# Rewriting the opening of a fused attention and FFN kernel engine by engine

## The chip, the cores and the metric

The kernel runs on one core of a Trainium2 chip. The core has a matrix engine (TensorE, PE in the profile), a vector engine (DVE), a scalar engine (ACT), GpSimd (POOL) and SyncE (SP), each with its own instruction queue that runs in order; 16 DMA engines move data. DMAs are issued by POOL (in software, the only kind here that converts fp32 to bf16 on the way) and by SP (in hardware). The metric is the time of one execution on the device in microseconds (us); lower is better. Three runs of the kernel before took 458.5, 458.74 and 458.5 us, so the median is 458.5.

## The reference

Attention over 8 batches, 12 heads, 448 positions and 64 columns a head, with a squared ReLU in place of the softmax; then a two-layer FFN with an exact GELU over the 3584 rows of 768 columns. Everything comes in and goes out in fp32.

```python
scores = scale * np.matmul(q, k.transpose(0, 1, 3, 2))      # scale = 1/8
attn = np.maximum(scores, 0.0) ** 2 / S                      # S = 448
x = np.matmul(attn, v)                                       # then heads side by side: 3584 x 768
h = x @ w_in                                                 # 768 x 2048
g = 0.5 * h * (1.0 + erf(h / np.sqrt(2)))
out = g @ w_out                                              # 2048 x 768
```

## The kernel before

**Layout.** The score matmul needs q and k with the head's 64 columns on the partitions (`qT`, `kT`, two heads side by side on 128 partitions). q and k arrive with positions on the partitions: `load` (line 71) issues on POOL, for a batch or for a quad of four heads, two DMAs of k into `nk`, one of q into `nq`, and two of v for each quad into `vt`. Each partition holds several neighbouring positions, so that the DMA's runs are long. `permute` (line 115) then copies `nk` to `pk` in two pieces (lines 127 and 128) and `nq` to `pq` (line 129), on DVE, which brings the columns of two heads together. After that they are transposed, in one of two ways:

- `prep_pe` (line 133), a quad at a time: the permutes, then eight PE transposes of k into one PSUM tile (line 140) that is copied to `kT` (by ACT at line 148 in batch 0, by DVE at line 150 otherwise), then eight of q, copied to `qT` by DVE (line 150). The PSUM tiles come from the pool `f_pp` with two buffers, which the FFN matmuls use too.
- `prep_dma` (line 152), a whole batch at a time: the permutes, then eight DMA transposes on SP, four of q and four of k (line 157).

`nk`, `nq`, `pk` and `pq` have one buffer each: the loads of the next batch wait for the permutes of the batch before, and the permutes wait for its transposes. `qT` and `kT` have two buffers.

**Steps.** A batch is 3 quads of 7 steps. `qk_step` (line 166) makes four score matmuls of 64 keys against 448 queries, one ReLU with the scale on ACT (line 181), and the square on DVE (line 183). `av_step` (line 186) makes four matmuls with v (line 193); after a quad's seventh step DVE copies the two PSUM banks to `xT` (line 204). These banks have two buffers in all, so the next quad's first `av_step` waits for the copies. The list `lag` holds the steps whose `av_step` is still to come.

**FFN.** `ffn1` (line 207) is one of 16 column blocks of the first product for one batch: 6 matmuls (line 212) and a GELU on ACT (line 219). `ffn2` (line 223) is half of one 128-row tile of the second product: 16 matmuls (line 228) and a copy on DVE (line 236); after the second half SP stores the tile (line 246).

**Order.** Every engine runs its instructions in the order in which the program emits them. `weave` (line 291) emits the score steps of a batch in pairs and puts FFN pieces ("atoms", with estimated costs 1.14 and 2.6) between the pairs in proportion; `prep` names what is emitted ahead of the pair that begins at step `l`. Batch 0 has no FFN work beside it (lines 324 to 337): one score step after the other, the `av_step` four steps behind. Batch 1 has the `ffn1` atoms of batch 0, batch b the `ffn1` atoms of b-1 and `ffn2` atoms of the pair of batches before.

**Preparation before the change.** Quad 0 of batch 0 is prepared at the start (line 323), quad 1 after step 1, quad 2 after step 5, quad 0 of batch 1 after step 16, each as one block: permutes, transposes, copies. Quads 1 and 2 of batch 1 are prepared in the same way ahead of steps 0 and 6 of batch 1's weave. Batch 2 is prepared by DMA transposes at the end of that weave (line 355), batch 3 ahead of step 12 of batch 2 (line 377), all later batches ahead of step 0 of the batch before (line 380), the loads of the batch after that ahead of step 4 (line 382).

Of the kernel before, what the change touches and what calls it, by code (L numbers as in the profile page):

```python
# [33 lines left out]
def kernel(  # L34
# [9 lines left out]
    nc = tc.nc  # L44
# [21 lines left out]
    f_pp = pool("f_pp", 2, PS)  # L66


    nq, nk, vt = {}, {}, {}

    def load(b, g0, g1):
# [6 lines left out]
        nc.gpsimd.dma_start(nk[b][:KB, h0:h1, :], kk[:, :, : 4 * D])  # L78
        nc.gpsimd.dma_start(nk[b][KB:, h0:h1, : 3 * D], kk[:, :, 4 * D :])  # L79
        nc.gpsimd.dma_start(  # L80
            nq[b][:, h0:h1, :], q[b, h0:h1].rearrange("h (p c) d -> p h (c d)", c=NC)
        )
        if b == 0 and g0 == 0:
            nc.gpsimd.affine_select(
                out=ident, in_=ident, compare_op=mybir.AluOpType.not_equal, fill=1.0,
                base=0, pattern=[[-1, 128]], channel_multiplier=1,
            )
# [27 lines left out]
    def permute(b, g0=0, g1=G):  # L115

        h0, h1 = 4 * g0, 4 * g1
# [5 lines left out]
        pq = perm[b][0].rearrange("p c (h d) -> p h c d", d=D)  # L123
        pk = perm[b][1].rearrange("p c (h d) -> p h c d", d=D)
        sq = nq[b].rearrange("p h (c d) -> p h c d", d=D)
        sk = nk[b].rearrange("p h (c d) -> p h c d", d=D)
        nc.vector.tensor_copy(pk[:, h0:h1, :3], sk[:, h0:h1, :3])  # L127
        nc.vector.tensor_copy(pk[:KB, h0:h1, 3], sk[:KB, h0:h1, 3])  # L128
        nc.vector.tensor_copy(pq[:, h0:h1], sq[:, h0:h1])  # L129

    ident = const.tile([128, 128], BF16, tag="ident", name="ident")

    def prep_pe(b, g):
        permute(b, g, g + 1)
        for w, rows in ((1, (128, 128, 128, 64)), (0, (KC,) * 4)):
            tp = f_pp.tile([128, 2, S], BF16, tag="f", name="tp")
            for j in range(2):
                off = 0
                for t, r in enumerate(rows):
                    nc.tensor.transpose(  # L140
                        tp[:, j, off : off + r],
                        perm[b][w][:r, t, bass.ts(2 * g + j, 128)],
                        ident[:r, :r],
                    )
                    off += r
            dst = get_T(b)[w][:, 2 * g : 2 * g + 2, :]
            if b == 0 and w == 1:
                nc.scalar.copy(dst, tp)  # L148
            else:
                nc.vector.tensor_copy(dst, tp)  # L150

    def prep_dma(b):
        permute(b)
        for w, rows in ((0, (KC,) * 4), (1, (128, 128, 128, 64))):
            off = 0
            for t, r in enumerate(rows):
                nc.sync.dma_start_transpose(  # L157
                    get_T(b)[w][:, :, off : off + r], perm[b][w][:r, t, :]
                )
                off += r  # L160
# [25 lines left out]
    def av_step(b, g, i):  # L186
        if i == 0:
            pav[b, g] = [av_pp.tile([128, NB], F32, tag="av", name="pav") for j in range(2)]
        a2 = asq.pop((b, g, i))
        for j in range(2):  # L190
            r = slice(64 * j, 64 * j + 64)
            for e in range(2):
                nc.tensor.matmul(  # L193
                    pav[b, g][j][64 * e : 64 * e + 64, :S],
                    vt[b][r, g, e, bass.ts(i, D)],
                    a2[r, e, :],
                    start=(i == 0),
                    stop=(i == NK - 1),
                )
# [49 lines left out]
    def f1(b):  # L249
        return [(1.14, ffn1, (b, m)) for m in range(KF)]  # L250
# [55 lines left out]
    def later(fn, *a):  # L306
        return lambda: fn(*a)
# [4 lines left out]

    nc.scalar.activation(warm, warm, AF.Gelu)
    load(0, 0, 1)
    load(0, 1, 2)
    load(0, 2, 3)
    load_win(0)
    load_win(1)

    ctx.enter_context(tc.manual_schedule())  # L320


    prep_pe(0, 0)
    for l, st in enumerate(steps(0)):
        qk([st])
        if l == 1:
            prep_pe(0, 1)
        if l == 5:
            prep_pe(0, 2)
            load(1, 0, 1)  # L330
            load_win(2)
            load(1, 1, 2)
            load_win(3)
            load(1, 2, 3)
        if l == 16:
            prep_pe(1, 0)
        run_av(4)


    s1, a0 = steps(1), f1(0)  # L340
    qk(s1[:2])
# [3 lines left out]
        s1[4:],  # L345
        a0[:14],
        {
            0: [later(prep_pe, 1, 1)],
            6: [
                later(prep_pe, 1, 2),  # L350
                later(load, 2, 0, G),
                later(load_wout, 0),
                later(load_wout, 1),
            ],
            16: [later(prep_dma, 2)],
        },
    )
    while lag:
        run_av(0)
    run(a0[14:])  # L360

    for b in range(2, B):
        x1, x2 = f1(b - 1), f2(b - 2)
        todo = steps(b)
        if b == 2:
            run(x1[:6])
            atoms = mix(x1[6:], x2)
        else:
            atoms = x2[:2] + mix(x1, x2[2:])
            if b % 2 == 0:  # L370
                todo = todo[1:]
            elif b + 1 < B:
                todo = todo + steps(b + 1)[:1]
        prep = {}
        if b == 2:
            load(3, 0, G)
            prep[12] = [later(prep_dma, 3), later(load, 4, 0, G)]
        else:
# [39 lines left out]
```

## Time and profile before

| | |
|---|---|
| median of three runs | 458.5 us |
| the profiled execution | 459.15 us |
| its span, first to last instruction | 457.4 us |
| mean granted clock of PE | 0.949 |
| PE busy | 401.9 us (88%) |
| DVE busy | 183.4 us (40%) |
| ACT busy | 212.6 us (46%) |
| POOL busy | 61.7 us (13%) |

The profile shows one execution. Its page groups the instructions; the trace behind it can be asked for stretches of time, single tiles, waits, and the chain of work that ended last. A line such as "82.18 9.26 PE L212 MATMUL psh<-xT,win_sb ... x48" says: from 82.18 us, over 9.26 us, 48 matmuls of line 212 that write `psh` and read `xT` and `win_sb`. A bracket at the end gives the idle time of the engine before that line and what ended it. SPq is the instruction queue of SP, where DMAs are issued; a line "DMA kT<-pk" is the transfer itself. The granted clock is the share of its full speed that PE was given: 1.00 is full, 0.50 half.

### The profile page before, as it was taken

To read this page: it belongs to the slowest core of one execution; us is meant where nothing else is said; L and a number is where in the kernel's file an instruction comes from. 1 tells how busy PE (TensorE), PEld (TensorE's weight loads), DVE (VectorE), ACT (ScalarE), POOL (GpSimd) and SP (SyncE) were. 2 spreads that over 40 slices of the span, in tenths; PEclk is the share of its full clock that TensorE was granted. 3 is DMA by queue.
4 is the path that set the end of the run, shared out by engine and by line. 5 is a ranking of instruction groups with operands and counts; after the bars stand their busy time and mean duration, and the time that the engine had idled before them with its cause. 6 is when DMAs were issued, how large, how long until landed. Compare 5 with 4: busy or idle time off the path is not lost.

```text
span 457.4 us, 7385 instructions
## 1 busy us (share of the span) xinstructions
PE 401.9 (88%) x3104; PEld 202.2 (44%) x3104; DVE 183.4 (40%) x319; ACT 212.6 (46%) x301; POOL 61.7 (13%) x95
## 2 busy tenths in 40 slices
PE   2677789804998599999999998999999999999995
PEld 1323344402543255445444544454545554455563
DVE  1566565201465253435434642464344344310021
ACT  2574467401555234655566464555555556412200
POOL 8361051410023040005000500000000000000000
PEclk9975899975999799999999999999999999999999
DMA  9999059997119999209951894135100201111122
GB/s 114 203 172 150 1 69 204 205 174 111 34 39 168 166 153 170 85 1 124 159 125 36 105 167 101 35 71 121 37 17 19 64 6 36 37 34 36 34 70 69
DMA packets 74049, 42.56 MB, mean 93 GB/s; under 512 B 42272, under 2 KB 70432, under 8 KB 74016
## 3 DMA queue, kind: packets, MB, share of 16 engines
q0 software_dynamic: 35744, 22.81, 36.0%
q1 hardware_dynamic: 38272, 19.28, 21.9%
q8 instruction: 24, 0.39, 0.4%
q14 instruction: 9, 0.07, 0.0%
HBM read 45.61 MB, written 11.01 MB: 124 GB/s over the span
## 4 chain that ended last, share of the span: by engine, by line
PE 64%; SPq 17%; DMA 8%; DVE 3%; issue 3%; ACT 3%; POOL 1%; DVEq 0%; ACTq 0%; POOLq 0%
PE pso L228 26%; PE psh L212 25%; SPq L157 16%; PE pav L193 7%; PE ps L173 5%; DMA kT<-pk 3%; ACT a_relu L181 3%; PE tp L140 2%; DMA v_sb<-in_v_dram 2%; DMA out_dram<-osb 2%; DMA nq<-in_q_dram 1%; DVE pq L129 1%; DVE pk L127 1%; DVE a_sq L183 1%; POOL nk L78 0%
## 5 line engine op out<-in xcount | busy, mean ns | idle before, releaser
L181 ACT ACTIVATE a_relu<-ps 128x896 bf16<-128x896 f32 x168 | 144.6, 916 | 147.6 <-PE ps L173 147.6
L212 PE MATMUL psh<-xT,win_sb 128*128 128x448 bf16 x768 | 156.4, 353 | 1.7 <-DVE osb L236 1.7
L228 PE MATMUL pso<-wout_sb,h_sb 128*128 128x384 bf16 x896 | 157.0, 332 | 0.0
L183 DVE TENSOR_TENSOR a_sq<-a_relu 128x896 bf16<-128x896 bf16 x168 | 104.4, 624 | 123.0 <-ACT a_relu L181 122.8
L228 PEld LDWEIGHTS <-h_sb 128*128 128x128 bf16 x896 | 87.5, 99 | 66.2 <-issue 11.1
L212 PEld LDWEIGHTS <-win_sb 128*128 128x128 bf16 x768 | 70.6, 98 | 81.3 <-issue 21.8
L219 ACT ACTIVATE h_sb<-psh 128x448 bf16<-128x448 f32 x128 | 70.0, 547 | 62.1 <-PE psh L212 62.1
L236 DVE COPY osb<-pso 128x384 f32<-128x384 f32 x56 | 31.2, 557 | 114.3 <-PE pso L228 106.0
L173 PE MATMUL ps<-qT,kT 64*64 64x448 bf16 x672 | 54.9, 382 | 24.2 <-DMA kT<-pk 22.1
L193 PE MATMUL pav<-a_sq,v_sb 64*64 64x448 bf16 x672 | 56.5, 389 | 7.7 <-DVE a_sq L183 4.6
L173 PEld LDWEIGHTS <-kT 64*64 64x64 bf16 x672 | 22.7, 113 | 41.7 <-DMA kT<-pk 23.8
L193 PEld LDWEIGHTS <-v_sb 64*64 64x64 bf16 x672 | 17.3, 111 | 38.2 <-issue 36.4
L78 POOL DMA_DIRECT2D nk<-in_k_dram x12 | 9.5, 792 | 175.1 <-DVE pk L128 174.3
L204 DVE CAST xT<-pav 128x448 bf16<-128x448 f32 x48 | 27.6, 617 | 11.6 <-PE pav L193 11.6
L91 POOL DMA_DIRECT2D v_sb<-in_v_dram x48 | 29.1, 633 | 14.6 <-DMA wout_sb<-in_moe_w_out_dram 7.8
L140 PE MATMUL tp<-ident,pk 128*128 128x128 bf16 (+1 forms) x48 | 7.1, 271 | 15.9 <-DVE pk L127 15.9
L140 PEld LDWEIGHTS <-pk 128*128 128x128 bf16 (+1 forms) x48 | 3.8, 113 | 21.0 <-DVE pk L127 18.5
L127 DVE COPY pk<-nk 128x768 bf16<-128x768 bf16 (+1 forms) x12 | 6.9, 575 | 11.3 <-DMA kT<-pk 7.2
L80 POOL DMA_DIRECT2D nq<-in_q_dram x12 | 10.1, 840 | 0.7 <-DMA nk<-in_k_dram 0.5
L129 DVE COPY pq<-nq 112x1024 bf16<-112x1024 bf16 (+1 forms) x12 | 8.6, 714 | 1.9 <-DMA nq<-in_q_dram 1.9
L79 POOL DMA_DIRECT2D nk<-in_k_dram x12 | 8.4, 699 | 3.1 <-DMA win_sb<-in_moe_w_in_dram 3.1
L148 ACT COPY kT<-tp 128x896 bf16<-128x896 bf16 x3 | 2.7, 905 | 9.4 <-PE tp L140 9.4
(16 smaller groups left out, 26.0 us busy)
## 6 DMA issues: line engine op xcount, KB each, us to landing
v_sb<-in_v_dram POOLq DMA_DIRECT2D x48, 112.0 KB, 13.9
nq<-in_q_dram POOLq DMA_DIRECT2D x6, 672.0 KB, 14.4
win_sb<-in_moe_w_in_dram POOLq DMA_DIRECT2D x4, 768.0 KB, 10.3
wout_sb<-in_moe_w_out_dram POOLq DMA_DIRECT2D x2, 1536.0 KB, 17.3
out_dram<-osb SPq DMA_DIRECT2D x8, 336.0 KB, 2.8
nk<-in_k_dram POOLq DMA_DIRECT2D x6, 384.0 KB, 6.0
out_dram<-osb SPq DMA_DIRECT2D x8, 288.0 KB, 2.6
out_dram<-osb SPq DMA_DIRECT2D x8, 240.0 KB, 2.8
```

Of the source, the lines that this page charges most:

```text
L91: nc.gpsimd.dma_start(vt[b][64 * j : 64 * j + 64, g], vv[g, j])
L140: nc.tensor.transpose(tp[:, j, off : off + r], perm[b][w][:r, t, bass.ts(2 * g + j, 128)], ident[:r, :r],)
L157: nc.sync.dma_start_transpose(get_T(b)[w][:, :, off : off + r], perm[b][w][:r, t, :])
L173: nc.tensor.matmul(ps[64 * j : 64 * j + 64, e, :S], kT[r, 2 * g + j, kcol(i) : kcol(i) + KB], qT[r, 2 * g + j, :], start=True, stop=True,)
L181: nc.scalar.activation(ar, ps[:, :, :S], AF.Relu, scale=c_att)
L183: nc.vector.tensor_mul(a2, ar, ar)
L193: nc.tensor.matmul(pav[b, g][j][64 * e : 64 * e + 64, :S], vt[b][r, g, e, bass.ts(i, D)], a2[r, e, :], start=(i == 0), stop=(i == NK - 1),)
L204: nc.vector.tensor_copy(xT[b][:, 2 * g + j, :], pav[b, g][j][:, :S])
L212: nc.tensor.matmul(ph[:, :S], win_sb[:, kd, bass.ts(m, 128)], xT[b][:, kd, :], start=(kd == 0), stop=(kd == KD - 1),)
L219: nc.scalar.activation(hT[b // 2][:, m, (b % 2) * S : (b % 2 + 1) * S], ph[:, :S], AF.Gelu)
L228: nc.tensor.matmul(po[:, :ND], hT[pr][:, kf, bass.ts(t, 128)], wout_sb[:, kf, bass.ts(n, ND)], start=(kf == 0), stop=(kf == KF - 1),)
L236: nc.vector.tensor_copy(osb[:, bass.ts(n, ND)], po[:, :ND])
```

## The change

The preparation is cut into its parts, and these are emitted at different steps.

- **The first q.** The four heads of q for quad 0 of batch 0 are no longer loaded by POOL with conversion. SP loads them in fp32 into a new tile `q32`; ACT copies them with conversion straight into `pq`. The quad's q is transposed first and copied by ACT, then k is permuted, transposed, and copied by DVE.
- **Batch 0.** `quad_prep` puts a quad's permute of k after one step, that of q after the next, the transposes of k three steps after the first and those of q four steps after it. It is used for quad 1 (from step 1), quad 2 (from step 6) and quad 0 of batch 1 (from step 15). In batch 0 ACT copies `kT`; in batch 1 DVE does.
- **Loads.** The `affine_select` that makes the identity for the transposes follows all loads of the first quad. Quarter 1 of the first weight is loaded after the first quad of batch 1. The loads of batch 1 are emitted after step 7.
- **Batch 1's weave.** `quad` (permutes) and `quad_T` (transposes) of quads 1 and 2 stand one pair of steps apart.
- **Batch 2** is prepared by PE transposes: quad 0 in batch 1's weave, quads 1 and 2 permuted there too and transposed ahead of steps 2 and 6 of batch 2. In batch 2's weave the first eight `ffn1` atoms go before the mix, where six were run ahead of the weave.
- **Later batches** keep the DMA transposes, k before q; they are emitted ahead of step 2 (step 10 in batch 2) instead of 0 (12), the loads ahead of step 10 (18 in batch 2) instead of 4 (12).

```diff
@@ load
-        nc.gpsimd.dma_start(
-            nq[b][:, h0:h1, :], q[b, h0:h1].rearrange("h (p c) d -> p h (c d)", c=NC)
-        )
-        if b == 0 and g0 == 0:
-            nc.gpsimd.affine_select(
...
+        qq = q[b, h0:h1].rearrange("h (p c) d -> p h (c d)", c=NC)
+        if b > 0 or g0 > 0:
+            nc.gpsimd.dma_start(nq[b][:, h0:h1, :], qq)
+        else:
+            nc.sync.dma_start(q32, qq)
@@ prep_pe and prep_dma become
+    def transpose_pe(b, g, w, copy):
+        tp = f_pp.tile([128, 2, S], BF16, tag="f", name="tp")
+        for j in range(2):
...
+                nc.tensor.transpose(
...
+        copy(get_T(b)[w][:, 2 * g : 2 * g + 2, :], tp)
+
+    def transpose_dma(b):
+        for w in (1, 0):
...
                 nc.sync.dma_start_transpose(
@@ the opening
+    V, A = nc.vector.tensor_copy, nc.scalar.copy
+    pq0 = get_perm(0)[0].rearrange("p c (h d) -> p h c d", d=D)
+    nc.scalar.copy(pq0[:, :4], q32.rearrange("p h (c d) -> p h c d", d=D))
+    transpose_pe(0, 0, 0, A)
+    permute_k(0, 0, 1)
+    transpose_pe(0, 0, 1, V)
+
+    def quad_prep(l0, b, g, copy_k):
+        return {
+            l0: [later(permute_k, b, g, g + 1)],
+            l0 + 1: [later(permute_q, b, g, g + 1)],
+            l0 + 3: [later(transpose_pe, b, g, 1, copy_k)],
+            l0 + 4: [later(transpose_pe, b, g, 0, V)],
+        }
+
+    def loads1():
+        load(1, 0, 1)
+        load_win(1)
+        load(1, 1, 2)
+        load_win(2)
+        load(1, 2, 3)
+        load_win(3)
+
+    prep0 = {**quad_prep(1, 0, 1, A), **quad_prep(6, 0, 2, A), **quad_prep(15, 1, 0, V)}
+    prep0[7].append(loads1)
     for l, st in enumerate(steps(0)):
         qk([st])
-        if l == 1:
-            prep_pe(0, 1)
...
         run_av(4)
+        for p in prep0.get(l, ()):
+            p()
@@ weave of batch 1
-            0: [later(prep_pe, 1, 1)],
+            0: [later(quad, 1, 1)],
+            2: [later(quad_T, 1, 1)],
             6: [
-                later(prep_pe, 1, 2),
+                later(quad, 1, 2),
...
-            16: [later(prep_dma, 2)],
+            8: [later(quad_T, 1, 2)],
+            14: [later(quad, 2, 0)],
+            16: [later(quad_T, 2, 0), later(quad, 2, 1), later(quad, 2, 2)],
         },
     )
+    load(3, 0, G)
@@ batches 2 to 7
         if b == 2:
-            run(x1[:6])
-            atoms = mix(x1[6:], x2)
+            atoms = x1[:8] + mix(x1[8:], x2)
...
         if b == 2:
-            load(3, 0, G)
-            prep[12] = [later(prep_dma, 3), later(load, 4, 0, G)]
-        else:
-            if b + 1 < B:
-                prep[0] = [later(prep_dma, b + 1)]
-            if b + 2 < B:
-                prep[4] = [later(load, b + 2, 0, G)]
+            prep[2] = [later(quad_T, 2, 1)]
+            prep[6] = [later(quad_T, 2, 2)]
+        nxt = []
+        if b + 1 < B:
+            nxt = [later(permute_k, b + 1), later(permute_q, b + 1), later(transpose_dma, b + 1)]
+        l = 10 if b == 2 else 2
+        prep[l] = nxt
+        if b + 2 < B:
+            prep[l + 8] = [later(load, b + 2, 0, G)]
         weave(todo, atoms, prep)
```

More of the change, by code (lines that the diff above doesn't have):

```diff
@@ L69 @@
     nq, nk, vt = {}, {}, {}
+    q32 = const.tile([KC, 4, NC * D], F32, tag="q32", name="q32")
     def load(b, g0, g1):
@@ L79, in load @@
         nc.gpsimd.dma_start(nk[b][KB:, h0:h1, : 3 * D], kk[:, :, 4 * D :])
-        nc.gpsimd.dma_start(
-            nq[b][:, h0:h1, :], q[b, h0:h1].rearrange("h (p c) d -> p h (c d)", c=NC)
-        )
-        if b == 0 and g0 == 0:
-            nc.gpsimd.affine_select(
-                out=ident, in_=ident, compare_op=mybir.AluOpType.not_equal, fill=1.0,
-                base=0, pattern=[[-1, 128]], channel_multiplier=1,
-            )
+        qq = q[b, h0:h1].rearrange("h (p c) d -> p h (c d)", c=NC)
[3 more added lines that the diff above has]
+            nc.sync.dma_start(q32, qq)
         vv = v[b].rearrange("(g j e) (p i) d -> g j p e (i d)", j=2, e=2, i=NK)
@@ L113, in get_T, with get_perm @@
         return qkT[b]
-    def permute(b, g0=0, g1=G):
-        h0, h1 = 4 * g0, 4 * g1
+    def get_perm(b):
         if b not in perm:
@@ L122, in permute, with permute_q, permute_k @@
             )
-        pq = perm[b][0].rearrange("p c (h d) -> p h c d", d=D)
-        pk = perm[b][1].rearrange("p c (h d) -> p h c d", d=D)
+        return perm[b]
+    def permute_q(b, g0=0, g1=G):
+        h = slice(4 * g0, 4 * g1)
+        pq = get_perm(b)[0].rearrange("p c (h d) -> p h c d", d=D)
         sq = nq[b].rearrange("p h (c d) -> p h c d", d=D)
+        nc.vector.tensor_copy(pq[:, h], sq[:, h])
+    def permute_k(b, g0=0, g1=G):
+        h = slice(4 * g0, 4 * g1)
+        pk = get_perm(b)[1].rearrange("p c (h d) -> p h c d", d=D)
@@ L126, in permute @@
         sk = nk[b].rearrange("p h (c d) -> p h c d", d=D)
-        nc.vector.tensor_copy(pk[:, h0:h1, :3], sk[:, h0:h1, :3])
-        nc.vector.tensor_copy(pk[:KB, h0:h1, 3], sk[:KB, h0:h1, 3])
-        nc.vector.tensor_copy(pq[:, h0:h1], sq[:, h0:h1])
+        nc.vector.tensor_copy(pk[:, h, :3], sk[:, h, :3])
+        nc.vector.tensor_copy(pk[:KB, h, 3], sk[:KB, h, 3])
     ident = const.tile([128, 128], BF16, tag="ident", name="ident")
[L133 to L148, printed above, removed]
-            else:
-                nc.vector.tensor_copy(dst, tp)
@@ L152, in prep_dma @@
-    def prep_dma(b):
-        permute(b)
-        for w, rows in ((0, (KC,) * 4), (1, (128, 128, 128, 64))):
-            off = 0
-            for t, r in enumerate(rows):
+    ROWS = ((KC,) * 4, (128, 128, 128, 64))
+    def transpose_pe(b, g, w, copy):
+        tp = f_pp.tile([128, 2, S], BF16, tag="f", name="tp")
+        for j in range(2):
+            off = 0
+            for t, r in enumerate(ROWS[w]):
+                nc.tensor.transpose(
+                    tp[:, j, off : off + r],
+                    perm[b][w][:r, t, bass.ts(2 * g + j, 128)],
+                    ident[:r, :r],
+                )
+                off += r
+        copy(get_T(b)[w][:, 2 * g : 2 * g + 2, :], tp)
@@ L157, in prep_dma @@
+    def transpose_dma(b):
+        for w in (1, 0):
+            off = 0
+            for t, r in enumerate(ROWS[w]):
                 nc.sync.dma_start_transpose(
@@ L314 @@
     load(0, 0, 1)
+    nc.gpsimd.affine_select(
+        out=ident, in_=ident, compare_op=mybir.AluOpType.not_equal, fill=1.0,
+        base=0, pattern=[[-1, 128]], channel_multiplier=1,
+    )
     load(0, 1, 2)
@@ L317, with quad, quad_T @@
     load_win(0)
-    load_win(1)
     ctx.enter_context(tc.manual_schedule())
-    prep_pe(0, 0)
+    V, A = nc.vector.tensor_copy, nc.scalar.copy
[20 more added lines that the diff above has]
+    prep0[7].append(loads1)
     for l, st in enumerate(steps(0)):
         qk([st])
-        if l == 1:
-            prep_pe(0, 1)
[L328 to L336, printed above, removed]
-        run_av(4)
+        run_av(4)
+        for p in prep0.get(l, ()):
+            p()
+    def quad(b, g):
+        permute_k(b, g, g + 1)
+        permute_q(b, g, g + 1)
+    def quad_T(b, g):
+        transpose_pe(b, g, 1, V)
+        transpose_pe(b, g, 0, V)
     s1, a0 = steps(1), f1(0)
```

1 line of the change is left out of this document (removed).

## The prediction

> **What bounds the kernel now.** First the stages: the view of busy time by window, whose columns are the window and its length, then busy time of PE, PEld, DVE, ACT and POOL with instruction counts, the granted clock, the DMA share and GB/s. The first line is the page's.
>
> ```profile
> span 457.4 us, 7385 instructions
> ...
> 30.00:40.00 10.00, 7.28 (x66) 3.39 (x59) 5.61 (x11) 5.61 (x7) 2.98 (x5) 0.50 1.30 194
> ...
> 80.00:100.00 20.00, 9.76 (x56) 4.72 (x51) 2.94 (x6) 5.34 (x10) 6.18 (x9) 0.92 1.27 190
> 100.00:110.00 10.00, 1.34 (x9) 0.40 (x10) 0.62 (x1) 1.03 (x2) 0.00 (x0) 0.50 1.23 178
> ...
> 200.00:300.00 100.00, 98.75 (x802) 49.53 (x804) 45.55 (x77) 54.74 (x78) 12.39 (x18) 1.00 0.65 98
> ```
>
> From 200 on PE is busy 98.75 of 100: nothing but less PE work helps there. The time to win lies earlier: between 80 and 110 PE is busy 11.1 of 30, and in the opening no engine is full. So I read those two places in order of time. Around batch 2 (start, length, what; the bracket is the idle time before and its releaser):
>
> ```profile
> 81.26 11.66 SPq L157 DMA_TRANSPOSE qT<-pq  x4
> ...
> 81.87 0.38 PE L193 MATMUL pav<-a_sq,v_sb 64*64 64x448 bf16 x4 [1.68 <-DVE a_sq L183]
> 82.18 9.26 PE L212 MATMUL psh<-xT,win_sb 128*128 128x448 bf16 x48
> ...
> 92.96 12.08 SPq L157 DMA_TRANSPOSE kT<-pk  x4
> ...
> 104.47 0.59 PE L173 MATMUL ps<-qT,kT 64*64 64x448 bf16 x4 [13.04 <-DMA kT<-pk]
> ...
> 109.24 0.59 PE L173 MATMUL ps<-qT,kT 64*64 64x448 bf16 x4 [4.18 <-DMA kT<-pk]
> ...
> 109.76 4.80 PE L228 MATMUL pso<-wout_sb,h_sb 128*128 128x384 bf16 x16
> ...
> 133.48 0.75 DVE L127 COPY pk<-nk 128x2304 bf16<-128x2304 bf16 x1
> ...
> 135.43 8.66 SPq L157 DMA_TRANSPOSE qT<-pq  x4
> ...
> 144.13 12.40 SPq L157 DMA_TRANSPOSE kT<-pk  x4
> ...
> 156.00 0.59 PE L173 MATMUL ps<-qT,kT 64*64 64x448 bf16 x4 [4.71 <-DMA kT<-pk]
> ...
> 157.31 7.51 PE L228 MATMUL pso<-wout_sb,h_sb 128*128 128x384 bf16 x32
> ```
>
> Batch 2's eight DMA transposes take from 81.26 to 109.2, and PE has work only until 91.4. It then waits 13.04 and 4.18. Batch 3's set ends late too: 4.71. After both waits the clock is at half: 16 matmuls of the second FFN product take 4.80 and 32 take 7.51, where 32 in a steady batch take 5.37:
>
> ```profile
> 209.69 5.37 PE L228 MATMUL pso<-wout_sb,h_sb 128*128 128x384 bf16 x32
> ...
> 253.51 5.37 PE L228 MATMUL pso<-wout_sb,h_sb 128*128 128x384 bf16 x32
> ```
>
> In the opening ACT sets the pace, one relu per attention step. The relus of the first 25 steps, and the first FFN matmul after them:
>
> ```profile
> 10.56 1.73 ACT L181 ACTIVATE a_relu<-ps 128x896 bf16<-128x896 f32 x2 [2.65 <-PE ps L173]
> ...
> 16.01 3.35 ACT L181 ACTIVATE a_relu<-ps 128x896 bf16<-128x896 f32 x4 [0.49 <-PE ps L173]
> ...
> 23.41 4.96 ACT L181 ACTIVATE a_relu<-ps 128x896 bf16<-128x896 f32 x6 [0.86 <-PE ps L173]
> 30.34 4.16 ACT L181 ACTIVATE a_relu<-ps 128x896 bf16<-128x896 f32 x5 [1.96 <-PE ps L173]
> 38.55 1.73 ACT L181 ACTIVATE a_relu<-ps 128x896 bf16<-128x896 f32 x2 [4.06 <-PE ps L173]
> 42.23 3.35 ACT L181 ACTIVATE a_relu<-ps 128x896 bf16<-128x896 f32 x4 [1.96 <-PE ps L173]
> 46.17 1.73 ACT L181 ACTIVATE a_relu<-ps 128x896 bf16<-128x896 f32 x2 [0.59 <-PE ps L173]
> ...
> 52.87 2.44 PE L212 MATMUL psh<-xT,win_sb 128*128 128x448 bf16 x12
> ```
>
> The relus add up to 21.0. Between them lie 3.72 (12.29 to 16.01), 4.05 (19.36 to 23.41), 1.97, 4.05, 1.95 and 0.59: 16.3 in all. The three long ones are a quad's preparation done in one block; the two of 1.96 are quad changes, where PE waits for DVE to empty the two attention banks.
>
> **The opening, part by part.**
>
> ```profile
> 1.25 0.74 POOL nk L78
> ...
> 2.58 5.07 DMA nq<-in_q_dram
> ```
>
> ```profile
> 5.03 0.61 DVE L127 COPY pk<-nk 128x768 bf16<-128x768 bf16 x1 [4.09 <-DMA nk<-in_k_dram]
> 5.57 0.20 DVE L128 COPY pk<-nk 64x256 bf16<-64x256 bf16 x1
> ...
> 9.93 0.96 PE L173 MATMUL ps<-qT,kT 64*64 64x448 bf16 x8 [0.71 <-DVE qT L150]
> ...
> 21.64 0.91 ACT L148 COPY kT<-tp 128x896 bf16<-128x896 bf16 x1 [2.29 <-PE tp L140]
> ...
> 35.07 0.35 DVE L127 COPY pk<-nk 128x768 bf16<-128x768 bf16 x1
> ...
> 35.47 0.41 DVE L129 COPY pq<-nq 112x1024 bf16<-112x1024 bf16 x1
> ...
> 37.64 0.62 DVE L150 COPY qT<-tp 128x896 bf16<-128x896 bf16 x1 [0.24 <-PE tp L140]
> ```
>
> ```profile
> out_dram<-osb SPq DMA_DIRECT2D x8, 336.0 KB, 2.8
> ```
>
> ```profile
> 35.48 2.12 PE tp L140 x16
> ...
> 61.84 1.38 PE tp L140 x16
> ```
>
> First q. It was issued third on POOL, at 2.58, and took 5.07. Now SP issues it at once (I put 1.0; POOL's first issue is at 1.25). No fp32 load on SP is in the trace: 2.8 for 336 KB written on SP is one end, q's own 5.07 the other. I take 3.6 (2.8 by 448/336 is 3.7), so it lands at 4.6. ACT's cast of 1024 columns costs 1.04 (0.91 for 896), to 5.65; ACT has nothing else waiting. The eight q transposes are some 0.95 of the 2.12 above (half clock), to 6.6; those of k, ready by 5.8, end at 7.7; DVE's copy, 0.62, at 8.35. First score matmul 8.4 against 9.93: 1.5 won (0 if q takes 5.07; 2.3 if 2.8, as k then decides). POOL loses one issue, so all later loads go that much earlier; the identity's select moves behind two issues of v, still ahead of the first transpose.
>
> A rule of the skill speaks against this edit. The Trainium skill, DMA: Bandwidth & Descriptors, section "Issuing engines are not separate DMA queues", says that DMAs of all issuers share the 16 engines, and another issuer saves only the time to initiate. By that rule q keeps its 5.07 and lands near 6.1, and the opening wins nothing here, 1.5 less.
>
> Then the steps. The permutes (0.35 + 0.20 + 0.41 a quad) run on DVE two or three steps before their transposes, so PE no longer stands through them. What remains: PE's 2.12 per quad between steps, which half clock leaves little room for (7.28 of 10 busy at 30 to 40); ACT's copy of kT, 0.91, in the row of relus for batch 0's quads; the quad changes, 1.96. Quad 1: 2.12 + 0.91, less 0.4 in PE's gaps: 2.6. Quad 2: the q transposes (0.95) lie inside the quad change: 2.12 + 0.91 + 1.96 - 0.95 - 0.4: 3.7. Quad 0 of batch 1: 2.12 + 1.96, and 0.62 for k's copy, now on DVE: 4.7. Together 11.0 instead of 16.3: 5.3 won. Ends: 5.7 of stalls if full clock hides all transposes (two changes, two copies), and 16.3 if the cover fails. If a load is late, DVE stands at its permute with all squares behind it, and ACT and PE behind those; before, no permute of quads 1 and 2 waited for a load, so I take nothing.
>
> After the 25th relu it took 4.97 (47.90 to 52.87) to the first FFN matmul, with quad (1,1) prepared in it. Now a square, the bank copies, two score steps: 2.5 (1.5 to 4.97). So the first FFN matmul comes at 10.56 - 1.5 + 21.0 + 11.0 + 2.5 = 43.6, **9.3 won**. Quads (1,1) and (1,2) then cost their PE time, 1.38 each; before, the second cost 1.38 and as much waiting for DVE. I count 0 (1.4 either way).
>
> The loads of batch 1 stand on POOL at step 7 but go as soon as the k permute frees their buffer, as before. Quarter 1 of the first weight moves behind batch 1's first quad; its first use is the fifth FFN product, some 5 after 43.6, so the move is hidden by all of batch 0.
>
> **Batch 2.** Eight transposes leave SP. The waits 13.04 + 4.18 go, and so does the half clock behind them, 4.80 - 2.69 = 2.1. Added on PE: quads (2,1) and (2,2), 2 x 1.38 = 2.8. At step 16 of batch 1 quad (2,0) adds 1.4, and DVE then has two copies and two quads of permutes (1.24 + 1.9) ahead of the square for the last attention step: PE waits some 2.2 for the 1.68 of before. That place loses 1.9 (1.4 to 4). Batch 3's set starts two steps sooner, at step 10, with its loads still beside it (they are released by the permute, whatever their place). From 133.48 it took 23.1 to land; five and a half pairs at 4.3 (43.8 from 209.69 to 253.51, ten pairs) give 23.7. Taken: 4.71 shrinks to 0.5, and 7.51 - 5.37 = 2.1 goes. Sum: 17.2 + 2.1 - 2.8 - 1.9 + 4.2 + 2.1 = 20.9. From the end of the last FFN matmul of batch 0 (84.5) to 157.31 are 72.9; less waits and clock 48.8, while a steady even batch of about two steps less takes 43.8: some small waits of thin stages go too, 1.9 taken (0 to 3.7). **22.8 won.**
>
> Here PE pays with transposes, and the page gives their mean record:
>
> ```profile
> L140 PE MATMUL tp<-ident,pk 128*128 128x128 bf16 (+1 forms) x48 | 7.1, 271 | 15.9 <-DVE pk L127 15.9
> ```
>
> The records overlap: 16 in 1.38 are 86 ns apart. The Trainium skill, TensorE: Matmul & The Clock Gate, section "Part 4: PE-mode transpose", gives about 275 ns for one in a kernel and says such work doesn't count as busy for the clock. As a latency the trace bears the 275 out; by it as a cost, a quad would take 4.4, and the sum would be 12 more for the four quads that are new on PE's path.
>
> **Later batches.** Transposes at step 2 instead of 0, k before q. A set takes 21 beside loads, a batch 43.8; first stores go ahead of it on SP. I count 0. The end is unchanged.
>
> **Sum.** 457.4 - 9.3 - 22.8 = 425.3. The profiled execution took 459.15, 1.75 above its span and 0.65 above the median 458.5: 427.05, or 426.4 beside that median. **I forecast 426.**
>
> **Rivals.**
> - *The opening keeps its stalls*: the clock stays at half, DVE and PE wait for each other in order, or q lands at 6.1. For it: 0.50 from 30 to 40. Against: the permutes leave the path. Stalls 16.3: 5.3 more, **431**, with q late 433. Mirror case: dense work brings full clock, **421**.
> - *Batch 3's set stays exposed*: the stage is 0.6 longer than the set. A set like batch 2's (28 from 81.26 to 109.2) would leave 4 and the half clock, 2.1: **432**.
> - *A transpose costs its record*: 16 x 0.271 = 4.3 for 1.38, 3.0 more in four added quads on PE's path: **438**. The row of 1.38 speaks against. This is the skill's figure taken as a cost.
> - *Slower*: the five sets of batches 3 to 7 become exposed, since they now begin a pair later on SP, behind stores. A set has some 39 from step 2 to the batch's end and takes 21. The point is 39; to eat 32, each must exceed it by 6.4, so last over 45; at 47 it is 426 + 5 x 8 = **466**. The worst set in the trace took 28.
>
> **Chances.** Forecast 0.62, opening worse 0.15, opening at full clock 0.09, batch 3's set 0.08, transposes 0.03, slower 0.02, and 0.01 for an edit without effect. Range 417 to 435: the forecast's ends, the mirror case and the two milder rivals. About 0.2% (0.9 us) can be told from no change: faster 0.97, same 0.01, slower 0.02.
>
> **What would show it.** First score matmul near 8.4 (q's cast on ACT before 6); relus of batch 0 broken by gaps of at most 3; first FFN matmul near 43.6; 40 DMA transposes instead of 48, none before 95; no PE wait above 2.5 between 65 and 120; the 32 matmuls that start batch 3 near 127, in 5.4; steady batches of 43.8. Wrong if PE waits for kT at batch 3's start by over 3, if DVE stands at a permute for a load, or if the first FFN matmul comes after 48.

## The result, and the profile after

The changed kernel takes 423.64 us (median of four runs, 422.86 to 426.11) against 458.5: a ratio of 0.9248, with a 95% interval of 0.9208 to 0.9288. The profiled execution took 422.99, with a span of 421.0. The forecast was 426, with a range of 417 to 435.

First the stages, in the same view as before the change (window, length, busy PE, PEld, DVE, ACT and POOL, granted clock, DMA share, GB/s):

```profile
30.00:40.00 10.00, 7.34 (x76) 3.26 (x76) 7.40 (x14) 5.66 (x7) 3.37 (x5) 0.83 1.34 197
...
80.00:100.00 20.00, 19.63 (x175) 10.19 (x178) 9.77 (x17) 10.28 (x15) 1.19 (x2) 1.00 0.80 124
100.00:110.00 10.00, 10.00 (x89) 5.02 (x80) 5.35 (x10) 4.69 (x7) 6.20 (x9) 1.00 1.02 116
...
200.00:300.00 100.00, 100.00 (x808) 50.02 (x807) 47.39 (x80) 55.77 (x80) 6.20 (x9) 1.00 0.52 87
```

From 80 to 110 PE is now busy 29.6 of 30 instead of 11.1. From 200 to 300 it has lost even the 1.25 that it still waited. PE's order of work at the milestones (the score matmul is line 172 now, the first FFN product 211, the second 227):

```profile
8.93 0.96 PE L172 MATMUL ps<-qT,kT 64*64 64x448 bf16 x8 [0.72 <-DVE kT L150]
...
41.25 2.44 PE L211 MATMUL psh<-xT,win_sb 128*128 128x448 bf16 x12
...
72.53 0.38 PE L192 MATMUL pav<-a_sq,v_sb 64*64 64x448 bf16 x4 [2.06 <-DVE a_sq L182]
72.84 2.44 PE L211 MATMUL psh<-xT,win_sb 128*128 128x448 bf16 x12
75.22 0.57 PE L172 MATMUL ps<-qT,kT 64*64 64x448 bf16 x8
...
124.60 5.37 PE L227 MATMUL pso<-wout_sb,h_sb 128*128 128x384 bf16 x32
```

The queue of SP has no set for batch 2 any more, and batch 3's set has been issued by 119.3. Its last transpose starts at 117.1 and lands 6.5 later, at 123.6; PE asks for it at 124.1:

```profile
0.74 0.38 SPq L85 DMA_DIRECT2D q<-in_q_dram  x1
...
100.39 6.04 SPq L156 DMA_TRANSPOSE kT<-pk  x4
106.48 12.85 SPq L156 DMA_TRANSPOSE qT<-pq  x4
```

And the relus of the first 25 steps on ACT, with the cast of q and the copies between them:

```profile
4.53 1.04 ACT L329 CAST pq<-q 112x1024 bf16<-112x1024 f32 x1 [2.30 <-DMA q<-in_q_dram]
...
9.57 4.16 ACT L180 ACTIVATE a_relu<-ps 128x896 bf16<-128x896 f32 x5 [2.07 <-PE ps L172]
14.35 0.91 ACT L150 COPY kT<-tp 128x896 bf16<-128x896 bf16 x1 [0.63 <-PE tp L144]
15.15 0.92 ACT L180 ACTIVATE a_relu<-ps 128x896 bf16<-128x896 f32 x1
16.64 0.92 ACT L180 ACTIVATE a_relu<-ps 128x896 bf16<-128x896 f32 x1 [0.56 <-PE ps L172]
18.05 2.54 ACT L180 ACTIVATE a_relu<-ps 128x896 bf16<-128x896 f32 x3 [0.49 <-PE ps L172]
20.61 0.91 ACT L150 COPY kT<-tp 128x896 bf16<-128x896 bf16 x1
21.41 1.73 ACT L180 ACTIVATE a_relu<-ps 128x896 bf16<-128x896 f32 x2
24.71 5.78 ACT L180 ACTIVATE a_relu<-ps 128x896 bf16<-128x896 f32 x7 [1.57 <-PE ps L172]
33.19 0.92 ACT L180 ACTIVATE a_relu<-ps 128x896 bf16<-128x896 f32 x1 [2.70 <-PE ps L172]
34.90 0.92 ACT L180 ACTIVATE a_relu<-ps 128x896 bf16<-128x896 f32 x1 [0.79 <-PE ps L172]
35.99 3.35 ACT L180 ACTIVATE a_relu<-ps 128x896 bf16<-128x896 f32 x4 [0.18 <-PE ps L172]
```

The gaps between them (1.42, 0.57, 0.49, 0.82, 1.57, 2.70, 0.79, 0.17) add up to 8.5; before they were 16.3. The 36.4 us of the two spans divide as follows, by milestones of the two traces:

| stretch | before | after | won | forecast |
|---|---|---|---|---|
| start to first FFN matmul | 52.87 | 41.25 | 11.6 | 9.3 |
| to the end of batch 0's FFN products | 84.5 - 52.87 | 75.22 - 41.25 | -2.3 | -1.9 |
| to the 32 matmuls that start batch 3 | 157.31 - 84.5 | 124.60 - 75.22 | 23.4 | 22.6 |
| from there to the end | 457.4 - 157.31 | 421.0 - 124.60 | 3.7 | 2.1 |

(The forecast's 22.8 for batch 2 is the sum of the last three rows. 84.5 is the end of the first 12 of the 48 matmuls at 82.18.) The first row is that of a favourable execution: in six traces whose opening is the same, the first FFN matmul comes between 41.25 and 43.27; more on this below.

### The profile page after: what moved, and what is told of

Read it like the earlier page. It is cut to its first block, busy times and chain, and to the rows that moved or that the text cites. A ratio compares the mean times of both kernels' runs of the same rounds, so it can differ in the third digit from the quotient of the medians.

```text
span 421.0 us, 7489 instructions
## 1 busy us (share of the span) xinstructions
PE 395.6 (94%) x3152; PEld 200.8 (48%) x3152; DVE 186.1 (44%) x330; ACT 213.3 (51%) x302; POOL 60.9 (14%) x94
## 4 chain that ended last, share of the span: by engine, by line
PE 87%; DVE 5%; ACT 4%; issue 2%; DMA 1%; POOL 0%; ACTq 0%; DVEq 0%; POOLq 0%
PE pso L227 35%; PE psh L211 34%; PE pav L192 9%; PE ps L172 7%; ACT a_relu L180 4%; PE tp L144 2%; DVE a_sq L182 2%; DMA nk<-in_k_dram 1%; DVE xT L203 1%; DVE qT L150 1%; DVE kT L150 0%; DVE pk L132 0%; DVE pq L126 0%; POOL nk L79 0%; DVE osb L235 0%
## 5 line engine op out<-in xcount | busy, mean ns | idle before, releaser
L227 PE MATMUL pso<-wout_sb,h_sb 128*128 128x384 bf16 x896 | 152.8, 326 | 0.0
L227 PEld LDWEIGHTS <-h_sb 128*128 128x128 bf16 x896 | 86.3, 98 | 63.1 <-issue 5.9
L192 PE MATMUL pav<-a_sq,v_sb 64*64 64x448 bf16 x672 | 53.8, 370 | 10.0 <-DVE a_sq L182 5.2
L172 PE MATMUL ps<-qT,kT 64*64 64x448 bf16 x672 | 51.9, 368 | 4.1 <-ACT a_relu L180 2.8
L192 PEld LDWEIGHTS <-v_sb 64*64 64x64 bf16 x672 | 16.3, 107 | 38.7 <-issue 36.9
L172 PEld LDWEIGHTS <-kT 64*64 64x64 bf16 x672 | 21.2, 108 | 20.6 <-issue 9.3
L144 PE MATMUL tp<-ident,pq 112*128 112x112 bf16 x72 | 6.2, 241 | 5.6 <-ACT pq L329 5.6
L144 PE MATMUL tp<-ident,pk 128*128 128x128 bf16 x72 | 8.6, 232 | 0.4 <-DVE pk L132 0.4
L144 PEld LDWEIGHTS <-pk 128*128 128x128 bf16 x72 | 5.5, 101 | 5.5 <-DVE a_sq L182 1.2
L144 PEld LDWEIGHTS <-pq 112*128 112x128 bf16 x72 | 4.5, 112 | 7.4 <-ACT pq L329 5.6
## 6 DMA issues: line engine op xcount, KB each, us to landing
win_sb<-in_moe_w_in_dram POOLq DMA_DIRECT2D x4, 768.0 KB, 10.2
```

Source lines behind the costliest of these rows:

```text
L144: nc.tensor.transpose(tp[:, j, off : off + r], perm[b][w][:r, t, bass.ts(2 * g + j, 128)], ident[:r, :r],)
L172: nc.tensor.matmul(ps[64 * j : 64 * j + 64, e, :S], kT[r, 2 * g + j, kcol(i) : kcol(i) + KB], qT[r, 2 * g + j, :], start=True, stop=True,)
L192: nc.tensor.matmul(pav[b, g][j][64 * e : 64 * e + 64, :S], vt[b][r, g, e, bass.ts(i, D)], a2[r, e, :], start=(i == 0), stop=(i == NK - 1),)
L227: nc.tensor.matmul(po[:, :ND], hT[pr][:, kf, bass.ts(t, 128)], wout_sb[:, kf, bass.ts(n, ND)], start=(kf == 0), stop=(kf == KF - 1),)
```

## The experiments

Every kernel was timed beside the kernel before; the ratios are to that kernel, with 95% intervals. The kernels were timed in four sets, and the kernel before took 456.39 to 458.5 us in them, so a difference of 1 or 2 us between kernels of different sets is not shown by their times; there the traces decide. My theory was that two parts give the gain, each by what it takes off PE's path. The main rival was that one part gives it, or that they depend on each other through the loads.

**The parts by themselves.** The first kernel, e1, has the old load order and the old blocks in batch 0, and is as changed from batch 1's weave on. The second, e2, has the new opening up to batch 0's last step, and is as before from batch 1's weave on.

> The opening as before, all from batch 1's later steps on as changed. My theory: the gain of the profiled execution (36.4 us) is the sum of two parts that don't depend on each other. The opening won 11.6 (first FFN matmul 52.87 before, 41.25 after); so this kernel should have its first FFN matmul near 52.5 and take 458.5 - 24.8 = 434 us, between 432 and 436. Rival: the parts depend on each other (a later opening gives the loads of batch 2 and the second weight more room, or an earlier one makes them collide): 428 or less, or 440 or more.

> The opening as changed, all from batch 1's later steps on as before (batch 2 by eight DMA transposes on SP). My theory: the opening's 11.6 us are kept, the waits for batch 2's set stay 17 and for batch 3's set 4 to 5: 447 us (445 to 449). Rival: batch 2's set is held up by the loads beside it, which do not come earlier by as much; then the wait for kT grows by what the opening won, and the time stays at 455 to 458.

Measured: e1 429.66 us, ratio 0.9402 (0.9346 to 0.9457); e2 451.93, ratio 0.9871 (0.9809 to 0.9933). The shares of time saved, 6.0% and 1.3%, add up to 7.3%; the changed kernel saved 7.5% in its own measurement and 7.2% in a later one (0.9281, 0.9254 to 0.9307). The two intervals leave this sum uncertain by some 0.8% (3.8 us), so the traces say it better: the two profiled spans, 427.8 and 449.9, are 29.6 and 7.5 shorter than 457.4, together 37.1 where the changed kernel won 36.4; and from the first FFN matmul to batch 3 e1 takes 83.34, the changed kernel 83.35. So the parts add, as the theory says, and neither time lies where the rival had it. But both times miss what I wrote (432 to 436, and 445 to 449), because I put the border wrongly: quad (1,1)'s block belongs to batch 1's weave, so e1 has it mended and e2 doesn't. In e1 the first FFN matmul comes at 48.52 and not near 52.5, in e2 at 46.09 and not near 41.25:

```profile
48.52 2.44 PE L230 MATMUL psh<-xT,win_sb 128*128 128x448 bf16 x12
```

In e2 PE waits for batch 2's set nearly as long as before (13.04 and 4.18), in spite of the earlier start:

```profile
98.15 0.59 PE L189 MATMUL ps<-qT,kT 64*64 64x448 bf16 x4 [12.63 <-DMA kT<-pk]
102.58 0.59 PE L189 MATMUL ps<-qT,kT 64*64 64x448 bf16 x4 [3.85 <-DMA kT<-pk]
```

**The first q by SP.**

```diff
-        if b > 0 or g0 > 0:
-            nc.gpsimd.dma_start(nq[b][:, h0:h1, :], qq)
-        else:
-            nc.sync.dma_start(q32, qq)
+        nc.gpsimd.dma_start(nq[b][:, h0:h1, :], qq)
...
-    nc.scalar.copy(pq0[:, :4], q32...)
+    nc.scalar.copy(pq0[:, :4], nq[0]...[:, :4])
```

> All as changed, but the first quad's q is loaded by POOL with conversion, between k and v as before; ACT still copies it to pq. My theory: q lands near 7.6 instead of 4.5, k near 5.0 instead of 6.24; ACT's copy ends at 8.6, q's transposes at 9.6, k's at 10.8, DVE's copy at 11.4: first score matmul 2.5 us later than 8.93, and 426 us. Rival, from the rule that another issuer saves only the time to initiate: k and q together land no earlier than before, so the first score matmul comes at most 1 us later, near 9.9, and the time is 424 to 424.6.

Measured: 425.73, ratio 0.9315 (0.9252 to 0.9377); the profiled span is 423.5, 2.5 more than 421.0 at nearly the same clock (0.994 and 0.993); the two ratios by themselves don't tell the kernels apart. ACT waits for q 3.4 longer, while k is there 1.3 sooner (DVE's copy starts at 5.03 instead of 6.33):

```profile
5.03 0.36 DVE L128 COPY pk<-nk 128x768 bf16<-128x768 bf16 x1 [4.08 <-DMA nk<-in_k_dram]
...
7.91 1.04 ACT L325 COPY pq<-nq 112x1024 bf16<-112x1024 bf16 x1 [5.67 <-DMA nq<-in_q_dram]
...
11.74 0.96 PE L168 MATMUL ps<-qT,kT 64*64 64x448 bf16 x8 [0.71 <-DVE kT L146]
```

In the changed kernel k is there at:

```profile
6.33 0.56 DVE L132 COPY pk<-nk 128x768 bf16<-128x768 bf16 x1 [5.39 <-DMA nk<-in_k_dram]
```

e3's first score matmul comes 2.8 later than the 8.93 of the changed kernel; the theory said 2.5, the rival at most 1. The rule of the Trainium skill that the prediction weighed (DMA: Bandwidth & Descriptors, "Issuing engines are not separate DMA queues") holds for the pair: the last of k and q is there 1.6 sooner by SP (6.33 for 7.91), about the 1.86 by which q is issued sooner (0.74 for 2.60). What it leaves out is the order: q, whose cast and transposes come first here, was moved ahead of k. With q by POOL the new order of the transposes is a loss: the kernel before, k first, had its first score matmul at 9.93, e3 at 11.74. Against that kernel the early q is worth 1.0.

**k by SP too.**

```diff
             nc.sync.dma_start(q32, qq)
+            nc.sync.dma_start(k32[:KB], kk[:, :, : 4 * D])
+            nc.sync.dma_start(k32[KB:, :, : 3 * D], kk[:, :, 4 * D :])
...
-        a2 = apool.tile(..., name="a_sq", bufs=8)
+        a2 = apool.tile(..., name="a_sq", bufs=7)
```

> All as changed, but k of the first quad is loaded by SP in fp32 as well (DVE's permute converts), and there are seven buffers for the squares instead of eight, to make room. My theory: k was held up to 6.24 by POOL's slower start beside q (4.97 before); on SP k lands by 5.6, the first score matmul comes at 8.3 instead of 8.93, 0.6 us sooner: 423 us. Rival: all DMAs share the same engines, the bytes of k and q together land no sooner, and k behind q on SP lands near 6.2 or later: 423.6 or more.

Measured: 426.24, ratio 0.9298 (0.9267 to 0.933). The theory falls: k lands 6.1 after its issue and is there at 8.1, where I had 5.6 and the rival 6.2 or later.

```profile
8.11 0.69 DVE L336 CAST pk<-k 128x768 bf16<-128x768 f32 x1 [7.16 <-DMA k<-in_k_dram]
...
10.84 0.96 PE L175 MATMUL ps<-qT,kT 64*64 64x448 bf16 x8 [0.72 <-DVE kT L153]
```

q is there at the same time as before (ACT casts at 4.45), k 1.8 later than with POOL beside SP. My reading is that behind q on one queue k waits for it, and that from another queue it shares the time; whether it is the queue's doing or that of fp32 was not separated. The start is 1.9 later; the rest of this profiled run's longer span (425.0) comes with half clock in the opening and behind batch 1, seen in other kernels too (below). The seventh instead of the eighth buffer shows no wait in the trace.

**Steps instead of blocks.** The new q and all else stay; only the quads that are prepared in batch 0, quad (1,0) among them, go back into blocks, and the loads of batch 1 follow step 5.

```diff
-    prep0 = {**quad_prep(1, 0, 1, A), **quad_prep(6, 0, 2, A), **quad_prep(15, 1, 0, V)}
...
+        if l == 1:
+            prep_pe(0, 1)
+        if l == 5:
+            prep_pe(0, 2)
+            loads1()
+        if l == 16:
+            prep_pe(1, 0)
```

> All as changed, but in batch 0 the quads are prepared in one block each after steps 1, 5 and 16, as before (permutes, transposes and copies together). My theory: the gaps between the relus of the first 25 steps go back from 8.5 to about 16 us, PE falls to half clock for some stretch between 10 and 45, the first FFN matmul comes near 49, and the time is 431 us (429 to 433). Rival: the gaps of before came from the half clock and the late start and not from the blocks; then the first FFN matmul comes by 44 and the time is 424 to 427.

Measured: 429.34, ratio 0.9391 (0.9336 to 0.9445): 5.7 us more than 423.64, and the intervals of the two ratios don't touch. The first FFN matmul comes at 47.59, and the gaps between the relus are 15.6 again; two of the three long ones stand in these lines (11.29 to 14.96 and 18.31 to 22.36):

```profile
9.56 1.73 ACT L197 ACTIVATE a_relu<-ps 128x896 bf16<-128x896 f32 x2 [2.23 <-PE ps L189]
13.57 0.91 ACT L150 COPY kT<-tp 128x896 bf16<-128x896 bf16 x1 [2.28 <-PE tp L144]
14.96 3.35 ACT L197 ACTIVATE a_relu<-ps 128x896 bf16<-128x896 f32 x4 [0.49 <-PE ps L189]
20.59 0.91 ACT L150 COPY kT<-tp 128x896 bf16<-128x896 bf16 x1 [2.29 <-PE tp L144]
22.36 4.96 ACT L197 ACTIVATE a_relu<-ps 128x896 bf16<-128x896 f32 x6 [0.86 <-PE ps L189]
```

So the blocks made the gaps, not the late start: the first score matmul is at 8.92 here too. The rival's other half, the half clock, has a share in them that was not separated: quad 2's transposes took 1.26 and 0.93 here and 0.88 and 0.57 in the changed kernel's trace. But ahead of each of the three blocks PE waits 2.0 to 2.4 us for DVE's permute, and that the clock doesn't set.

**Where batch 3's set stands.**

```diff
-        l = 10 if b == 2 else 2
+        l = 12 if b == 2 else 2
```

The loads that follow stay at step 18.

> All as changed, but batch 3's permutes and DMA transposes are emitted ahead of step 12 of batch 2 instead of step 10, as before. My theory: with step 10 the set is issued by 119.4 and PE asks for it at 124.1; one pair later (4.7 us) it is issued at about 124.1 and PE waits 0.5 to 3 us for kT at the start of batch 3; 424 to 427 us. Rival: without batch 2's set and with the second weight long landed the set runs faster, and there is no wait: 423.6.

Measured: 429.6, ratio 0.9363 (0.9329 to 0.9397). PE waits 3.54 and then runs at half clock, so that the 32 matmuls take 7.05 instead of 5.37:

```profile
128.59 0.57 PE L172 MATMUL ps<-qT,kT 64*64 64x448 bf16 x8 [3.54 <-DMA qT<-pq]
```

The mechanism is right, but the time lies above the 424 to 427 that I wrote: the wait is a little over my 0.5 to 3, and I left out the clock, 1.7 more. The set's last transpose was issued 4.7 later, and it landed at 128.3; the changed kernel had only 0.5 in hand there (123.6 for 124.1). In the other kernels with the set at step 10 it is 0.1 to 1.3. One pair of steps is far more than the margin of this place.

**Where the later sets stand.**

```diff
-        l = 10 if b == 2 else 2
+        l = 10 if b == 2 else 0
```

> All as changed, but the sets of batches 4 to 7 are emitted ahead of step 0 instead of step 2 (loads two steps earlier as well). After the start of batch 3 the changed kernel won 3.7 us, of which 2.1 is the clock; my theory: the other 1.6 us are waits for the output stores behind the transposes on SP (DVE waited 8.3 us for stores before, and none now), so this kernel is 1 to 2 us slower, 424.6 to 425.6, and DVE's copy to osb waits for the store again. Rival: the waits went for another cause; time 423.6 and no such wait.

Measured: 425.46, ratio 0.9284 (0.9253 to 0.9314). By total time this can't be told from the changed kernel. By the trace it can: from the 32 matmuls of batch 3 (125.88) to the end (424.2) are 298.3, where the changed kernel and the other kernels with the same order there and no late set have 295.9 to 296.4. The lists of waits (in all, times, longest) show why. Before the change DVE waited for stores, and PE for DVE's copies behind them:

```profile
DVE osb L236 <- DMA out_dram<-osb: 8.3, 2, 4.5
...
PE psh L212 <- DVE osb L236: 1.7, 2, 1.2
```

The changed kernel has neither wait; e6 has both again:

```profile
DVE osb L235 <- DMA out_dram<-osb: 4.3, 1, 4.3
...
PE psh L211 <- DVE osb L235: 1.7, 2, 1.0
```

With the sets at step 2 the stores of the pair before go ahead of them on SP. This is the 1.6 that the forecast counted at nothing. (The loads, which e6 emits two steps earlier as well, were not tried by themselves.)

**PE's wait at the end of batch 1.** Three edits were tried at what the trace still shows.

```diff
 e7: permutes of quads (2,1) and (2,2) in batch 2's weave
-            16: [later(quad_T, 2, 0), later(quad, 2, 1), later(quad, 2, 2)],
+            16: [later(quad_T, 2, 0)],
...
+            prep[0] = [later(quad, 2, 1)]
+            prep[2] = [later(quad_T, 2, 1), later(quad, 2, 2)]
...
 e9: one FFN product ahead of the last attention step
+    run(a0[14:15])
     while lag:
         run_av(0)
-    run(a0[14:])
+    run(a0[15:])
 e10: quad (1,0) permuted after steps 12 and 13
+    prep0[12], prep0[13] = prep0.pop(15), prep0.pop(16)
```

> All as changed, but the permutes of quads 1 and 2 of batch 2 are emitted ahead of steps 0 and 2 of batch 2 (and the loads of batch 3 ahead of step 4) instead of at the end of batch 1. My theory: PE's wait of 2.06 us at 72.5 for the last square, which stands behind these permutes on DVE, falls to 0.5 to 1.0; 422 to 422.6 us. Rival: the permutes delay squares as much at the new places, or the later loads of batch 3 come late: 423.6 or more.

> All as changed, but one of the two first-FFN products that follow the last attention step of batch 1 is emitted ahead of it. My theory: PE's wait of 2.06 us for the last square falls to about 0.9 us (1.14 of product lies in it), nothing new waits, and the clock keeps full there in every run: 1.1 us less in the profile's stretch from the first FFN matmul to batch 3 (83.35 before, so 82.2), and a median 1 to 2 us lower. Rival: the wait reappears a step later, at the first product that reads batch 1's last banks: no gain.

> All as changed, but quad 0 of batch 1 is permuted after steps 12 and 13 instead of 15 and 16 (its transposes stay). My theory: in the changed kernel the bank copies after quad 1 stand behind these permutes and squares on DVE, which makes the longest gap between relus, 2.70 us; without them it is 1.8 to 2.0, and the first FFN matmul comes 0.7 to 0.9 us sooner: about 0.8 us less. Rival: the loads of that quad, issued from 18.9 on, aren't there at step 12 (about 26); DVE then stands at the permute and the gap moves to there: no gain or a loss.

> All as changed, with three edits: the permutes of quads 1 and 2 of batch 2 later, one FFN product ahead of batch 1's last attention step, the permutes of batch 1's quad 0 sooner. My theory: the gains add, 0.4 + 1.1 + 0.8: some 2.3 us less than the changed kernel, 421 to 422 us, and less spread since no wait over 1 us is left between 45 and 120. Rival: each wait that goes lets another one end last: at most 1 us.

> The changed kernel itself once more, beside the three below. Its four runs went from 422.86 to 426.11. My theory: they differ by the granted clock, which falls to half for a stretch of some 3.4 us or not, after PE's wait of 2.06 us near 72.5 and in the opening (a kernel with that wait showed 12 matmuls right behind it in 4.10 us, 1.65 more than the 2.44 here): 423 to 426 us again. Rival: the clock plays no part and the spread is the chip's; then runs of like clock differ by as much.

| kernel | median us | ratio, 95% | first FFN matmul to batch 3 |
|---|---|---|---|
| e7 | 423.39 | 0.9238 (0.9212 to 0.9265) | 82.96 |
| e9 | 423.4 | 0.926 (0.9234 to 0.9287) | 82.21 |
| e10 | 424.07 | 0.9297 (0.9261 to 0.9333) | 83.65 |
| e11, all three | 421.75 | 0.9234 (0.9206 to 0.9261) | 81.83 |
| changed kernel again | 423.96 | 0.9281 (0.9254 to 0.9307) | 84.97 |

(In e7 and e11 the loads of batch 3 move to step 4 too.) e9, e10, e11 and the changed kernel ran together. In the changed kernel's first profile the last column is 83.35. The wait of 2.06 falls to 1.68 in e7, where only the way from relu to square to `av_step` is left, to 0.81 in e9, where an FFN product fills it, and to 0.44 with both:

```profile
74.16 0.38 PE L192 MATMUL pav<-a_sq,v_sb 64*64 64x448 bf16 x4 [1.68 <-DVE a_sq L182]
```

```profile
74.39 0.38 PE L192 MATMUL pav<-a_sq,v_sb 64*64 64x448 bf16 x4 [0.81 <-DVE a_sq L182]
```

```profile
72.73 0.38 PE L192 MATMUL pav<-a_sq,v_sb 64*64 64x448 bf16 x4 [0.44 <-DVE a_sq L182]
```

For e7 I had expected 0.5 to 1.0 and a lower time; but the 1.68, the same as before the change, is the chain of relu (0.92) and square (0.63) behind the last score matmul, which no other order on DVE shortens. e9's stretch came out as expected (82.2), its median did not: 0.6 lower than that of the changed kernel beside it, where I had written 1 to 2. e10's theory falls: its longest gap between relus is 3.31 us, and e9, whose transposes there are as slow and whose permutes stand where they were, has 3.49. The permutes are worth 0.2 here and not 0.7 to 0.9, because DVE's bank copies wait for the square of step 17 whether or not permutes stand before it. e11 is faster than the kernel before and than the changed kernel: its runs (421.06 to 422.94) all lie below those of the changed kernel beside it (423.02 to 425.11), though the two intervals of the ratio still touch.

The changed kernel run again tells where its own spread comes from. After the same wait as at 72.53 above, the same 12 matmuls take 3.69 instead of 2.44:

```profile
73.16 0.38 PE L192 MATMUL pav<-a_sq,v_sb 64*64 64x448 bf16 x4 [2.05 <-DVE a_sq L182]
73.48 3.69 PE L211 MATMUL psh<-xT,win_sb 128*128 128x448 bf16 x12
```

From its first FFN matmul to batch 3 this costs 1.6 (84.97 for 83.35). The other traces with this order fall into the same two groups: e1, e3 and e6 at 83.34 to 83.35, e4 and e8, with the half clock behind the wait, at 84.95 to 85.0; e10 alone lies between. The opening has such a choice as well. In the changed kernel's first profile the transposes of k for quad 2 and quad (1,0) run at full pace:

```profile
19.69 0.88 PE L144 MATMUL tp<-ident,pk 128*128 128x128 bf16 x8
...
31.94 0.88 PE L144 MATMUL tp<-ident,pk 128*128 128x128 bf16 x8
```

In that of e9, whose opening is the same, they run at half pace, the gaps between the relus add up to 10.1 instead of 8.5, and the first FFN matmul is 1.9 later:

```profile
20.12 1.27 PE L144 MATMUL tp<-ident,pk 128*128 128x128 bf16 x8
...
33.21 1.27 PE L144 MATMUL tp<-ident,pk 128*128 128x128 bf16 x8
...
43.12 2.44 PE L211 MATMUL psh<-xT,win_sb 128*128 128x448 bf16 x12
```

The two profiles of the changed kernel differ by 2.2 (421.0 and 423.2): 0.6 in the opening, 1.6 in the stretch to batch 3, nothing behind it (296.4 and 296.3). By the mean clock alone the runs order themselves only roughly. The four earlier ones do (spans of 421.0 and 421.1 at 0.993, 422.5 at 0.987, 424.3 at 0.983); of the six later ones those at 0.982 and 0.983 are the longest (423.2) and the one at 0.993 the shortest (421.2), but the one at 0.985 took 421.4 and the one at 0.990 421.7. e11's five runs spread over 1.9 us and e9's six over 1.2, against 2.1 and 3.3 for the changed kernel; that few runs don't show that the spread is less.

## Why the prediction was right

**The mechanism held at both places, and the parts add** (e1, e2). By the steps of the sum:

- *The first q.* q landed at 4.5 (4.6 foreseen), the cast took 1.04, as worked out. But k came at 6.33 instead of 5.03: I had counted SP's early q as free for k, and it wasn't. Hence 8.93 and not 8.4; 1.0 won of 1.5, and less in other traces of the same opening (up to 9.57).
- *The stalls between relus.* 8.5 for 11.0. Quad 1 cost 2.5 (2.6 foreseen), quad 2 2.4 (3.7), quad (1,0) 3.7 (4.7). Most of this is the pace and so luck: I had put all transposes at half clock. In the profiles of e9 and e7 the eight of k take 1.23 to 1.27, the gaps add up to 10.1 and 10.2, quad 2 costs 3.3 and quad (1,0) 4.3 in e9, and the first FFN matmul comes at 43.12 and 43.27, near the 43.6 foreseen. So some 1.6 of the 2.5 is a part of my mirror case, which this execution happened to get, and 0.9 is a size that I put too high.
- *After the 25th relu.* 1.9 for 2.5.
- *The end of batch 1.* The wait for the last square was 2.06 (2.2 foreseen), in place of 1.68.
- *Batch 2.* Both waits and the half clock behind them went: 23.4 for 22.6. The transposes cost 1.2 to 1.4 a quad, as their row of 1.38 said; a price by record length, the rival from the Trainium skill, TensorE: Matmul & The Clock Gate, section "Part 4: PE-mode transpose", is out: 16 take 1.21 on the chain that ended last.
- *Batch 3's set* was not exposed, but only by 0.5 us (landed at 123.6, asked for at 124.1), where I had left 0.5 of wait; e5 shows that one pair later it is exposed. That rival was right as a mechanism and missed by little.
- *Later batches.* I counted 0, and this term was wrong: the stores that now go ahead gave 1.6, PE's two waits of 1.7 in all, and e6 takes 1.9 away again. The rival that ended slower saw the same two things on SP, stores and sets, and got the sign wrong.

By spans the forecast was 4.3 too high (425.3 for 421.0): 2.3 in the opening, 0.8 in batch 2 and 1.6 in the stores, less 0.4 at the end of batch 1. By the median it was only 2.4 too high, because the profiled execution was one of the faster runs; the opening's surplus is for the most part the luck of that execution.

## What to carry to other kernels

Preparation in one block costs the latency of its whole chain on every engine that stands in order behind it; spread over the steps, it costs only the engines' time, so look for which engine has that time free. A transfer that is just off the critical path is not settled: find its margin, from its landing and not from its issue, since past it you pay the wait and then the clock. A gain read from one profile holds that execution's luck with the clock: compare the same stretch in several. Where two transfers feed one start, moving one ahead takes time from the other, so order them by the length of what follows each.

## What the runs showed of the hardware

- A wait of PE of 2.05 us was enough, in some executions and not in others, to bring the half clock right behind it (12 matmuls in 3.67 to 4.10 instead of 2.44). The Trainium skill, TensorE: Matmul & The Clock Gate, section "What's actually happening", gives an idle window of about 3.4 us for this; shorter gaps did it here. PE had little other work around the gap: from 69.05 to 73.48 of the changed kernel's later run stand 16 transposes, 16 short matmuls and the wait. Whether transposes count as work no run here shows.
- The granted clock reads 1.00 in the first 20 us of the changed kernel's trace, but PE runs there at the pace that goes with 0.50 elsewhere: four score matmuls take 0.59 up to 18 (and 0.59 from 26 to 30 of the later run, granted 0.50), and 0.38 from 20.5 on.
- A set of eight DMA transposes of one batch kept SP's queue busy for 10.5 us alone (batch 7's, 274.6 to 285.1) and for 18.9 to 21.3 beside a batch's loads.
- An fp32 load of 448 KB on SP landed 3.8 us after its issue, and the two loads of k beside it on POOL took 4.4 and 4.2 instead of 3.2 and 3.0.
